# Row transfers dealt by 32 cut into four of 32 partitions, and a block's raw rows moved to another buffer, in an adaLN block with linear attention and a SiLU MLP

## The chip, the cores and the metric

The kernel runs on one core of a Trainium2 chip. Five engines work side by side, each on its own instruction stream: TensorE (PE; its weight loads are listed apart as PEld), VectorE (DVE), ScalarE (ACT), GpSimd (POOL) and SyncE (SP), which in this kernel only issues DMA transfers. Engines and transfers are tied by semaphores. The metric is the device time of one execution in microseconds (us); the median of the runs shown counts.

## The reference

All arrays are float32. With S = 2048 rows, D = 576, H = 32 heads of 18, F = 4608:

```python
mod = (_silu(c) @ w_mod).reshape(1, 6, 1, -1)
sa, ca, ga, sb, cb, gb = (mod[:, j] for j in range(6))

h = _layernorm(x) * (1 + ca) + sa
q, k, v = heads(h @ wqkv)                      # 576 -> 3 * 576
phi = lambda t: where(t > 0, t + 1, exp(t)) + 1e-6
kv  = einsum("bhsd,bhse->bhde", phi(k), v)
z   = einsum("bhsd->bhd", phi(k))
o   = einsum("bhqd,bhde->bhqe", phi(q), kv) / (einsum("bhqd,bhd->bhq", phi(q), z) + 1e-6)
x   = x + ga * (o @ wo)

h = _layernorm(x) * (1 + cb) + sb
x = x + gb * (silu(h @ w1) @ w2)               # 576 -> 4608 -> 576
```

## The kernel before, in words

**Stages.** Four stretches follow each other. From 0 to about 35 us the first 512 rows are normalised and turned, and the first modulation (sa, ca) is made. From there to about 251 us runs the *block stage*, with which most of the change has to do. To about 400 us the attention is finished and the MLP begun, and then the MLP streams its weights past two halves ("pairs") of the rows until 1125 us. The last stretch adds what is left and stores the output.

**The block stage.** The 2048 rows form four blocks of 512, and a block four tiles of 128. The rows of a block must come as columns for PE's products: element d of row s has to stand in partition d mod 128. For block 0 TensorE transposes them. For blocks 1 to 3 it goes through VectorE and DRAM (`block_steps`, from L899):

1. L902 loads four row tiles into `xt` (128 partitions x 4 x 576). They are *dealt by 32*: partition 32a + j of tile t holds row 128a + 32t + j of the block. `rows_of` (L331 to L335) gives that view of DRAM, with shape [4, 32, 576].
2. LayerNorm: statistics on DVE (L242, L243, 0.44 us each half row), small steps (L907 and L909 on DVE, a power on POOL in L908), and the normalised rows, again in `xt`: two tiles by DVE, two by ACT.
3. Four DVE transposes of 32 x 32 squares (L916), from `xt` to `sq`, which is the fourth accumulator buffer `accb[3]` ("acc" in the profile).
4. `store` (L922) writes `sq` to DRAM in four transfers; `fetch_main` (L928) and `fetch_tail` (L933) read it back, four transfers each of 32 partitions, into `xT` (in `accb[2]`) and `tail` (the profile calls it h32 or hT).
5. `turn_steps` modulates, and splits each piece into a high half (ACT, L896) and a low half (DVE, L897) in `hT`, whose products PE makes.

PE then projects k and q of the block (L846): `k_steps` gives phi(k) through an exponential on ACT (L852), L853 and L406 on DVE, and splits it into high and low parts (L861, L864). `split_rows` (L875, L877, L879) does the same with the normalised rows in `xt`, and `sum_steps` (L951) multiplies the two, summing phi(k)^T x over all rows. `xt` is therefore read until the sums' operands are split, and only then free for the next block's rows.

**The second modulation.** `mod_steps` runs beside this, once for (ga, sb) and once for the last pair: weight rows come in (L346), ACT scales them (L992, L994), POOL adds five pieces into `tmod` (L995), L996 writes the 128 partial sums to DRAM, L999 gathers them back turned (9-element runs), DVE adds them up (L1002) and L1003 writes the vector out.

**What sets the order.** The block stage is written down as a list of steps in `Schedule` (L734), each with an engine, a duration, a lag for transfers, and the names that it reads and writes. PE keeps the order of the list. On the other engines, SP among them, the planner runs the list with the given durations: the step that can begin earliest goes, and of several the one with the earliest due time. The names make the dependences: a step that writes a name comes after all that read it. `SQ` names the four parts of `sq`, `XT` those of `xT`. So the given durations change no instruction, only the order on DVE, ACT, POOL and SP. The stretch before it and the one from 251 us on have orders written out as numbers (`FIRST`, `ORDERS`): the n-th instruction of an engine within the stretch. The MLP has a planner list of its own.

**Queues.** All large transfers go out on SP's queue in order: an issue that has to wait for its data, or for a transfer issued eight earlier to land, holds up those behind it. Three other places use rows dealt by 32: q_scale (L716) and q_norm (L731), which load a tile of x into the accumulator after q has been used (12 dealt tiles of blocks 1 to 3, and 4 of block 0, which are not dealt); `store` of the MLP's first pair (L1910), half a row each; and `plain_store` (L1930) of the second pair at the end, behind `plain_add` (L1925).

Names in the profile: `big` and `small` are PSUM tiles of the first stretch, `psK` those of the projections, `psG` of the sums, `up` and `down` those of the MLP; `as_`/`a` is phi(k), `pk` its split form (shown as w in places), `xs` the split rows.

Of the kernel before, what the change touches and what calls it, by code (L numbers as in the profile page):

```python
# [18 lines left out]
P = 128  # L19
EPS_LN = 1e-5  # L20
EPS = 1e-6
# [3 lines left out]
def kernel(ctx: ExitStack, tc, A_x, A_wqkv, A_wo, B_x, B_w1, B_w2, c, w_mod, out):  # L25
# [33 lines left out]
    def behind(instructions):  # L59

        with ExitStack() as order:
# [30 lines left out]
        "SP": """  # L92
            2-4 0-1 6-7 5 8-10 13 11-12 14-16 23 20 18 17 19 25-26 22 24 21 27-30 32 31 34-35 33 38 47 37 39-40
            36 41-45 48-49 51 50 46
        """,
# [234 lines left out]

    def rows_of(y, t, c=slice(0, D)):  # L331
        b = t // 4
        if b == 0:
            return y[t * P : (t + 1) * P, c]
        return y[b * 512 : (b + 1) * 512, c].rearrange("(a t j) d -> t a j d", a=4, t=4)[t % 4]  # L335

# [374 lines left out]
    def q_scale(t, pn):  # L711
        a, r = acc[t], rs_of.pop(t)
        G.tensor_mul(pn[:, :D].rearrange("p (h d) -> p h d", d=DH), a.rearrange("p (h d) -> p h d", d=DH),
                     r.unsqueeze(2).to_broadcast([P, H, DH]))
        G.tensor_copy(pn[:, D:], pn[:, KC * P : D])
        nc.sync.dma_start(a, rows_of(x, t))  # L716

    rs_of = {}

    def q_norm(t, prod, pn):  # L720

        a = acc[t]
# [7 lines left out]
        G.tensor_copy(pn[:, D:], pn[:, KC * P : D])  # L730
        nc.sync.dma_start(a, rows_of(x, t))  # L731
        return pn
# [117 lines left out]

    def phi_steps(ps, k, out, names):
        do("ACT", 0.65, lambda: A.activation(halves(e_), ps[:, :, :HALF], AF.Exp), [k], ["e"])  # L852
        do("DVE", 0.75, lambda: V.tensor_scalar(halves(out), ps[:, :, :HALF], 0.0, EPS, op0=ALU.max, op1=ALU.add), [k], names)  # L853
        do("DVE", 0.79, lambda: phi_out(e_, out), ["e"], names)

    def k_steps(t):
        ps, k = project(t, wkp)
        i, n = t % 4, t % 2
        a, an = as_[n], f"a{n}"
        phi_steps(ps, k, a, [an])  # L860
        do("ACT", 0.68, lambda: A.copy(pk[i][:, 0], a), [an], [f"pkh{i}"])  # L861
        by_pool = i < 2 or t == 2
        eng, us = (G, 1.6) if by_pool else (V, 0.75)
        do("POOL" if by_pool else "DVE", us, lambda: eng.tensor_sub(pk[i][:, 1], a, f32(pk[i][:, 0])), [an, f"pkh{i}"], [f"pkl{i}"])  # L864
        do("POOL", 1.6, lambda: G.tensor_add(zsum, zsum, a), [an], ["zsum"])
# [5 lines left out]
    def split_rows():  # L871

        C = KC * P
        for t in range(4):
            do("ACT", 0.68, lambda t=t: A.copy(xs[t][:, :D], xt[:, t, :D]), [f"xt{t}"], [f"xhi{t}"])  # L875
            eng, us = (V, 0.7) if t < 2 else (G, 1.35)
            do("DVE" if t < 2 else "POOL", us, lambda t=t, eng=eng: eng.tensor_sub(xs[t][:, DX:], xt[:, t, :C], f32(xs[t][:, :C])),  # L877
               [f"xt{t}", f"xhi{t}"], [f"xlo{t}"])
            do("DVE", 0.17, lambda t=t: V.tensor_sub(xs[t][:, D:DX], xt[:, t, C:D], f32(xs[t][:, C:D])), [f"xt{t}", f"xhi{t}"], [f"xtl{t}"])  # L879

# [6 lines left out]
    def turn_steps(b):  # L887

        for k in START:
# [7 lines left out]
            do("DVE", 0.69, lambda src=src, lo=lo, hi=hi: V.tensor_sub(dealt(hT[b][:, lo, :]), taken(src), dealt(f32(hT[b][:, hi, :]))), [name, hs[0]], [hs[1]])  # L897

    def block_steps(b):  # L899

        for t in range(4):
            do("SP", 0.1, lambda t=t: nc.sync.dma_start(xt[:, t, :D], rows_of(x, 4 * b + t)), [], [f"xt{t}"], 6.5)  # L902
        for t in range(4):
            do("DVE", 1.1, lambda t=t: ln.stats(t, xt[:, t, :D]), [f"xt{t}"], [f"mv{t}"])
        for u in (0, 2):
            ve, rstd, nm = (t[:, u : u + 2] for t in (ln.ve, ln.rstd, ln.nm))
            do("DVE", 0.17, lambda u=u, ve=ve: V.tensor_scalar(ve, ln.mv[:, u : u + 2, 1], EPS_LN, None, op0=ALU.add), [f"mv{u}", f"mv{u + 1}"], [f"ve{u}"])  # L907
            do("POOL", 1.0, lambda u=u, ve=ve, rstd=rstd: G.tensor_tensor(rstd, ve, neghalf[:, u : u + 2], op=ALU.pow), [f"ve{u}"], [f"rstd{u}"])  # L908
            do("DVE", 0.17, lambda u=u, rstd=rstd, nm=nm: V.scalar_tensor_tensor(nm, ln.mv[:, u : u + 2, 0], -1.0, rstd, op0=ALU.mult, op1=ALU.mult), [f"rstd{u}"], [f"nm{u}"])  # L909
        for t in range(4):  # L910
            eng, us = (A, 0.86) if t % 2 else (V, 0.58)
            row = xt[:, t]
            do("ACT" if t % 2 else "DVE", us, lambda t=t, eng=eng, row=row: ln.normalise(t, row, row, eng, ((0, 0, D),)), [f"nm{t // 2 * 2}"], [f"xt{t}"])
        s3 = sq.rearrange("p (f q) -> p f q", q=P)
        for t in range(4):
            do("DVE", 0.76, lambda t=t: V.transpose(s3[:, :, 32 * t : 32 * t + 32], xt[:, t, :D].rearrange("p (f i) -> p f i", i=32)),  # L916
               [f"xt{t}"], [f"sq{t}"])
        room = turned[b - 1]
# [145 lines left out]
    def load_late():  # L1064
        for cc in range(NHC):
            n = HG if cc < NHC - 1 else TAIL
            do("SP", 0.1, lambda cc=cc, n=n: nc.sync.dma_start(wos[cc][:n], A_wo[cc * HG : cc * HG + n, :]), [], [wo_names[cc]], 6.0)
            do("DVE", 0.75, lambda cc=cc, n=n: V.tensor_mul(wos[cc][:n], wos[cc][:n], bc["ga"][:n]), ["bcga"], [wo_names[cc]])
        do("SP", 0.6, lambda: [load_rows(wvs[k], A_wqkv[:, 2 * D : 3 * D], k) for k in START], [], [*SQ, "raw1.1"], 8.0)
# [97 lines left out]
    q_steps(3)  # L1167
    turn_steps(1)
    split_rows()
    block_steps(2)  # L1170
# [4 lines left out]
    for c in START:  # L1175
        sum_steps(1, c)
    turn_steps(2)
    split_rows()
    block_steps(3)
# [583 lines left out]
    class Unit:  # L1763
# [164 lines left out]
        def plain_store(self, t, *ks):  # L1928
            a, c = 8 * self.pair + t, slice(ks[0] * HALF, (ks[-1] + 1) * HALF)
            nc.sync.dma_start(rows_of(of, a, c), acc[a][:, c])  # L1930

# [359 lines left out]
```

## Time and profile before

| what | value |
|---|---|
| runs of the kernel before | 1157.32, 1157.75, 1158.25 us (median 1157.75) |
| profiled execution, its own time | 1158.3 us |
| its span in the trace | 1156.6 us |
| mean granted TensorE clock | 0.972 |
| PE, PEld busy | 1080.4, 773.2 us |
| DVE, ACT, POOL busy | 915.8, 695.6, 722.1 us |
| moved by DMA | 193.52 MB, 167 GB/s over the span |
| block stage | 35 to 251 us |
| last stretch | 1125 to 1156.6 us |

How to read it: a group of instructions shows its line, engine, operation, tiles written and read, shape, count, then the busy time and the mean duration in ns, then the idle time of the engine just before them and what ended most of it. `SPq` is the issue of a transfer on SP's queue; its duration contains the time for which the issue stood there. A row of the chain of work gives a start, a length and what ran. A row of waits says which instruction waited on which, then the total in us, the count and the longest.

### The profile page before, as it was taken

The page shows a single profiled execution, that of the slowest core. Times are in us where ns is not written, and L with a number is a line of the kernel's source. Part 1 is how long each engine was busy: PE and PEld are TensorE (multiplying, and loading weights), DVE is VectorE, ACT ScalarE, POOL GpSimd, SP SyncE. Part 2 cuts the span into 40 slices and gives each one's busy share as a digit, 9 for nine tenths or more (in the row PEclk, how much of TensorE's full clock was granted, in tenths as well). Part 3 has the DMA queues.
Part 4 walks back from the last instruction along what each step waited for, and adds up shares of the span by engine and source line. Part 5 has one row for each costly group of instructions (what it writes and reads, how often), then busy time and mean ns, then how long its engine had stood idle before and what let it go on. Part 6 is the DMA issues. An engine that isn't in the chain of part 4 may idle for free.

```text
span 1156.6 us, 19138 instructions
## 1 busy us (share of the span) xinstructions
PE 1080.4 (93%) x7027; PEld 773.2 (67%) x7027; DVE 915.8 (79%) x1467; ACT 695.6 (60%) x1300; POOL 722.1 (62%) x789
## 2 busy tenths in 40 slices
PE   8888696999999997899999999999999999999993
PEld 7888696999888554466666666666666666666662
DVE  7768494858698889979898788887887987987672
ACT  5553334333856568767676587686676776756460
POOL 2335161435472568957979769778688777785570
PEclk9989799999999999999999999999999999999997
DMA  7353949314334575858757848747657567446312
GB/s 240 103 141 103 131 115 174 106 54 109 120 98 141 180 245 165 278 127 255 206 172 237 235 124 268 221 127 255 210 154 250 189 183 223 169 126 207 109 62 82
DMA packets 119507, 193.52 MB, mean 167 GB/s; under 512 B 42928, under 2 KB 77748, under 8 KB 119412
## 3 DMA queue, kind: packets, MB, share of 16 engines
q1 hardware_dynamic: 119240, 191.99, 56.8%
q8 instruction: 55, 0.90, 0.3%
q14 instruction: 40, 0.33, 0.1%
q10 hardware_dynamic: 172, 0.30, 0.1%
HBM read 176.77 MB, written 15.48 MB: 166 GB/s over the span
## 4 chain that ended last, share of the span: by engine, by line
PE 74%; DVE 9%; DMA 6%; ACT 4%; SPq 2%; POOL 2%; issue 1%; DVEq 0%; ACTq 0%; POOLq 0%
PE up L1803 29%; PE down L1887 28%; PE big L295 6%; PE psK L846 2%; DMA xt<-in_A_x_dram 2%; DMA acc<-turned 2%; PE psG L951 1%; PE small L1311 1%; DMA turned<-acc 1%; PE big L1322 1%; SPq L928 1%; DVE hT L167 1%; PE psK L1116 1%; DVE a L406 1%; SPq L648 1%
## 5 line engine op out<-in xcount | busy, mean ns | idle before, releaser
L1803 PE MATMUL up<-hT,w 128*128 128x512 f16 x1264 | 317.7, 381 | 8.9 <-DMA hT<-hd 4.0
L1803 PEld LDWEIGHTS <-w 128*128 128x128 f16 x1492 | 146.3, 98 | 143.5 <-issue 11.3
L1896 DVE SCALAR_TENSOR_TENSOR acc<-acc,set,down 128x576 f32<-128x576 f32 x128 | 103.5, 810 | 34.3 <-PE down L1887 33.5
L1841 POOL TENSOR_TENSOR s<-f,f 128x256 f32<-128x256 f32 x66 | 55.1, 835 | 92.8 <-ACT f L1822 90.5
L1821 ACT ACTIVATE f<-f,set 128x512 f32<-128x512 f32 x102 | 73.3, 719 | 62.2 <-DVE f L1827 51.2
L1887 PE MATMUL down<-w,hb 128*128 128x288 f16 x600 | 88.9, 286 | 2.3 <-DVE U L1898 1.7
L1887 PE MATMUL down<-w,hc 128*128 128x288 f16 x600 | 88.9, 286 | 0.2 <-DVE acc L1900 0.2
L1887 PE MATMUL down<-w,hT 128*128 128x288 f16 x480 | 82.8, 286 | 0.4 <-DVE acc L1900 0.4
L1825 DVE TENSOR_TENSOR f<-up,p 128x512 f32<-128x512 f32 x102 | 69.6, 682 | 15.0 <-PE up L1803 9.7
L1822 ACT ACTIVATE f<-f,set 128x512 f32<-128x512 f32 x102 | 73.6, 722 | 3.3
L1887 PEld LDWEIGHTS <-hb 128*128 128x128 f16 x600 | 58.7, 98 | 24.3 <-issue 2.4
L1887 PEld LDWEIGHTS <-hc 128*128 128x128 f16 x600 | 58.7, 98 | 21.9 <-issue 0.5
L846 PE MATMUL psK<-w,hT 128*128 128x288 f32 x308 | 51.9, 322 | 21.5 <-ACT hT L896 13.1
L1827 DVE TENSOR_TENSOR f<-up,f 128x512 f32<-128x512 f32 x68 | 46.8, 688 | 25.7 <-PE up L1803 25.0
L1865 POOL TENSOR_TENSOR hc<-s,hc 128x512 f16<-128x512 f32 x50 | 63.2, 1264 | 5.6 <-ACT hc L1861 5.6
L1887 PEld LDWEIGHTS <-hT 128*128 128x128 f16 x480 | 47.0, 98 | 26.6 <-issue 0.8
L1845 POOL TENSOR_TENSOR f<-f,s 128x256 f32<-128x256 f32 x66 | 53.4, 810 | 17.2 <-DVE hb L1865 10.1
L846 PEld LDWEIGHTS psK<-w,hT 128*128 128x128 f32 x308 | 48.1, 212 | 22.7 <-ACT hT L896 13.5
L1838 POOL TENSOR_TENSOR s<-f 128x256 f32<-128x256 f32 x66 | 56.6, 857 | 7.9 <-ACT f L1818 4.8
L1843 POOL TENSOR_TENSOR s<-s,f 128x256 f32<-128x256 f32 x66 | 56.2, 852 | 3.4
L951 PE MATMUL psG<-w,xs 128*128 128x288 f32 x336 | 52.3, 313 | 2.6 <-DVE sum L961 2.5
L1887 PE MATMUL down<-w,hd 128*128 128x288 f16 x396 | 54.7, 287 | 0.0
(396 smaller groups left out, 2800.5 us busy)
## 6 DMA issues: line engine op xcount, KB each, us to landing
hT<-hd SPq DMA_DIRECT2D x101, 640.0 KB
hT<-hd SPq DMA_DIRECT2D x65, 512.0 KB
hT<-in_B_w_dram SPq DMA_DIRECT2D x14, 576.0 KB
hT<-in_B_w_dram SPq DMA_DIRECT2D x28, 256.0 KB
raw<-in_B_w_dram SPq DMA_DIRECT2D x9, 576.0 KB
v<-in_B_w_dram SPq DMA_DIRECT2D x9, 576.0 KB
xt<-in_A_x_dram SPq DMA_DIRECT2D x16, 288.0 KB
raw<-in_w_mod_dram SPq DMA_DIRECT2D x8, 576.0 KB
```

The costliest lines, as they stand in the source:

```text
L295: T.matmul(ps, xpart(a), wpart(b), start=n == 0, stop=n == len(XW) - 1)
L846: T.matmul(o, part(a), w(b), start=c == 0 and m == 0, stop=c == KC and m == 1)
L951: T.matmul(ps[:, h, :HALF], l, pk[t][:, u, h * HALF : (h + 1) * HALF], start=t == 0 and m == 0, stop=t == 3 and m == len(left) - 1)
L1803: T.matmul(ps, left, right, start=first and m == 0, stop=m == len(seq) - 1, skip_group_check=True)
L1821: A.activation(f, f, AF.Silu, scale=factor(self.g, "inv"))
L1822: aside(A.activation(f, f, AF.Identity, scale=factor(self.g, "delta")))
L1825: V.tensor_add(f, self.bank[bank[1]], self.p1)
L1838: G.tensor_sub(self.s3, half(i, 0, 0), half(i, 0, 1))
L1843: G.tensor_sub(self.s[:, 1:2], self.s[:, 0:1], half(i, 0, 0))
L1865: eng.tensor_sub(t[:, :, 1, :], src, t[:, :, 0, :])
L1887: T.matmul(ps[:, p, :HALF], left[:, u, p * P : (p + 1) * P], right[:, v], start=n in (1, 5, 7, 6) and j == 0, stop=j == len(passes) - 1, s ...
L1896: V.scalar_tensor_tensor(dst, dst, factor(self.g, "ratio"), ps[:, :, :HALF], op0=ALU.mult, op1=ALU.add)
```

## The change

The kernel after differs in four ways.

- **Pieces.** `rows_of` is gone. `pieces(t, n)` gives a list of pairs: a slice of 32 partitions, and the view of 32 rows in DRAM (or n tiles' rows) that belongs there. A transfer of dealt rows becomes four transfers of 32 partitions; block 0 keeps one of 128. This holds for the loads of x in `q_scale` and `q_norm` (`load_rows_of`), and for both stores of the output. `store` of pair 0 makes one transfer (block 0) or four (block 1) for two tiles, where it made two.
- **Room.** A block's raw rows no longer go to `xt` but to `row4`, the room `accb[3]` in which the turned squares will stand, in four transfers of 32 partitions x 4 tiles. Statistics and the normalising steps read them there; the normalised rows go to `xt` as before. Each transpose now writes all four names of `SQ`, since it overwrites room of any raw tile.
- **Place in the list.** Loads and statistics form `early_steps(b)`, which stands ahead of `split_rows()` in the list, and so ahead of the last readers of the block before.
- **Durations.** The planner's figures for many steps are others. The order string of SP has new numbers for the same order, with 36 more issues.

```diff
+    def pieces(t, n=1):
+        if t < 4:
+            return [(slice(0, P), lambda y: y[t * P : (t + n) * P].rearrange("(u p) d -> p u d", u=n))]
+        r0 = [t // 4 * 512 + a * P + t % 4 * 32 for a in range(4)]
+        return [(slice(32 * a, 32 * a + 32), lambda y, r=r: y[r : r + 32 * n].rearrange("(u j) d -> j u d", u=n))
+                for a, r in enumerate(r0)]
...
-        nc.sync.dma_start(a, rows_of(x, t))
+        load_rows_of(a, t)
...
+    def load_rows_of(a, t):
+        for p, rows in pieces(t):
+            nc.sync.dma_start(a[p], rows(x)[:, 0])
...
-        do("DVE", 0.79, lambda: phi_out(e_, out), ["e"], names)
+        do("DVE", 1.05, lambda: phi_out(e_, out), ["e"], names)
...
-        eng, us = (G, 1.6) if by_pool else (V, 0.75)
+        eng, us = (G, 1.52) if by_pool else (V, 1.1)
...
-            eng, us = (V, 0.7) if t < 2 else (G, 1.35)
+            eng, us = (V, 0.74) if t < 2 else (G, 1.55)
...
-    def block_steps(b):
+    def early_steps(b):
+        row4 = accb[NB - 1]
+        def load():
+            for p, rows in pieces(4 * b, 4):
+                nc.sync.dma_start(row4[p], rows(x))
+        do("SP", 0.3, load, [], SQ, 7.0)
         for t in range(4):
-            do("SP", 0.1, lambda t=t: nc.sync.dma_start(xt[:, t, :D], rows_of(x, 4 * b + t)), [], [f"xt{t}"], 6.5)
-        for t in range(4):
-            do("DVE", 1.1, lambda t=t: ln.stats(t, xt[:, t, :D]), [f"xt{t}"], [f"mv{t}"])
+            do("DVE", 1.1, lambda t=t: ln.stats(t, row4[:, t]), [f"sq{t}"], [f"mv{t}"])
...
+    def block_steps(b):
+        row4 = accb[NB - 1]
         for t in range(4):
-            eng, us = (A, 0.86) if t % 2 else (V, 0.58)
-            row = xt[:, t]
-            do("ACT" if t % 2 else "DVE", us, lambda t=t, eng=eng, row=row: ln.normalise(t, row, row, eng, ((0, 0, D),)), [f"nm{t // 2 * 2}"], [f"xt{t}"])
+            eng, us = (A, 0.87) if t % 2 else (V, 0.7)
+            do("ACT" if t % 2 else "DVE", us, lambda t=t, eng=eng: ln.normalise(t, xt[:, t], row4[:, t], eng, ((0, 0, D),)),
+               [f"nm{t // 2 * 2}", f"sq{t}"], [f"xt{t}"])
...
-               [f"xt{t}"], [f"sq{t}"])
+               [f"xt{t}"], SQ)
...
-        do("SP", 0.4, store, SQ, [f"turned{b}"], 4.7)
-        do("SP", 0.4, fetch_main, [f"turned{b}"], XT, 4.5)
-        do("SP", 0.4, fetch_tail, [f"turned{b}"], [XTAIL], 5.5)
+        do("SP", 0.4, store, SQ, [f"turned{b}"], 5.2)
+        do("SP", 0.4, fetch_main, [f"turned{b}"], XT, 5.0)
+        do("SP", 0.4, fetch_tail, [f"turned{b}"], [XTAIL], 6.0)
...
+    early_steps(1)
     split_rows()
     block_steps(1)
...
+    early_steps(2)
     split_rows()
     block_steps(2)
...
+    early_steps(3)
     split_rows()
     block_steps(3)
...
-            for u in range(2):
-                nc.sync.dma_start(rows_of(of, 4 * b + 2 * i + u, slice(k * HALF, (k + 1) * HALF)), self.c(b, i, k)[:, u])
+            for p, rows in pieces(4 * b + 2 * i, 2):
+                nc.sync.dma_start(rows(of[:, k * HALF : (k + 1) * HALF]), self.c(b, i, k)[p])
...
-            nc.sync.dma_start(rows_of(of, a, c), acc[a][:, c])
+            for p, rows in pieces(a):
+                nc.sync.dma_start(rows(of[:, c])[:, 0], acc[a][p, c])
```

In the order that the planner then writes, PE's instructions stand as before. Rows of block 1 are issued right behind the startup's last weight load (L302) and ahead of the weight rows of L648; those of blocks 2 and 3 right behind the fetch of the block before. The gather L999 (L1019 in the kernel after) of the first `mod_steps` is issued ahead of the second block's store instead of behind it, and on DVE the first statistics of blocks 2 and 3 stand ahead of some low halves of `hT`.

More of the change, by code (lines that the diff above doesn't have):

```diff
@@ L92 @@
         "SP": """
-            2-4 0-1 6-7 5 8-10 13 11-12 14-16 23 20 18 17 19 25-26 22 24 21 27-30 32 31 34-35 33 38 47 37 39-40
-            36 41-45 48-49 51 50 46
+            2-4 0-1 6-13 5 14-25 28-31 26-27 32-43 50-53 47 45 44 46 55-62 49 54 48 63-66 68 67 70-71 69 74 83
+            73 75-76 72 77-81 84-85 87 86 82
         """,
@@ L730, in q_norm @@
         G.tensor_copy(pn[:, D:], pn[:, KC * P : D])
-        nc.sync.dma_start(a, rows_of(x, t))
+        load_rows_of(a, t)
         return pn
@@ L849, in project, with phi_steps @@
         return ps, k
-    def phi_steps(ps, k, out, names):
+    def phi_steps(ps, k, out, names, by_act=False):
         do("ACT", 0.65, lambda: A.activation(halves(e_), ps[:, :, :HALF], AF.Exp), [k], ["e"])
-        do("DVE", 0.75, lambda: V.tensor_scalar(halves(out), ps[:, :, :HALF], 0.0, EPS, op0=ALU.max, op1=ALU.add), [k], names)
-        do("DVE", 0.79, lambda: phi_out(e_, out), ["e"], names)
+        if by_act:
+            do("ACT", 0.65, lambda: A.activation(halves(out), ps[:, :, :HALF], AF.Relu), [k], names)
+            do("ACT", 0.68, lambda: A.activation(out, out, AF.Identity, bias=eps), [], names)
+        else:
+            do("DVE", 0.75, lambda: V.tensor_scalar(halves(out), ps[:, :, :HALF], 0.0, EPS, op0=ALU.max, op1=ALU.add), [k], names)
+        do("DVE", 1.05, lambda: phi_out(e_, out), ["e"], names)
+    BY_ACT = ()
     def k_steps(t):
@@ L875, in split_rows @@
             do("ACT", 0.68, lambda t=t: A.copy(xs[t][:, :D], xt[:, t, :D]), [f"xt{t}"], [f"xhi{t}"])
-            eng, us = (V, 0.7) if t < 2 else (G, 1.35)
+            eng, us = (V, 0.74) if t < 2 else (G, 1.55)
             do("DVE" if t < 2 else "POOL", us, lambda t=t, eng=eng: eng.tensor_sub(xs[t][:, DX:], xt[:, t, :C], f32(xs[t][:, :C])),
                [f"xt{t}", f"xhi{t}"], [f"xlo{t}"])
-            do("DVE", 0.17, lambda t=t: V.tensor_sub(xs[t][:, D:DX], xt[:, t, C:D], f32(xs[t][:, C:D])), [f"xt{t}", f"xhi{t}"], [f"xtl{t}"])
+            do("DVE", 0.3, lambda t=t: V.tensor_sub(xs[t][:, D:DX], xt[:, t, C:D], f32(xs[t][:, C:D])), [f"xt{t}", f"xhi{t}"], [f"xtl{t}"])
     def dealt(y):
@@ L1067, in load_late @@
             do("SP", 0.1, lambda cc=cc, n=n: nc.sync.dma_start(wos[cc][:n], A_wo[cc * HG : cc * HG + n, :]), [], [wo_names[cc]], 6.0)
-            do("DVE", 0.75, lambda cc=cc, n=n: V.tensor_mul(wos[cc][:n], wos[cc][:n], bc["ga"][:n]), ["bcga"], [wo_names[cc]])
+            do("DVE", 1.1, lambda cc=cc, n=n: V.tensor_mul(wos[cc][:n], wos[cc][:n], bc["ga"][:n]), ["bcga"], [wo_names[cc]])
         do("SP", 0.6, lambda: [load_rows(wvs[k], A_wqkv[:, 2 * D : 3 * D], k) for k in START], [], [*SQ, "raw1.1"], 8.0)
```

11 lines of the change are left out of this document (3 added, 8 removed).

## The prediction

> **What bounds the kernel now.** I read the page first, then the busy time by stage, PE's own waits, the chain of work in order of time, and the queue of SP. The page:
>
> ```profile
> span 1156.6 us, 19138 instructions
> PE 1080.4 (93%) x7027; PEld 773.2 (67%) x7027; DVE 915.8 (79%) x1467; ACT 695.6 (60%) x1300; POOL 722.1 (62%) x789
> PE up L1803 29%; PE down L1887 28%; PE big L295 6%; PE psK L846 2%; DMA xt<-in_A_x_dram 2%; DMA acc<-turned 2%; PE psG L951 1%; PE small L1311 1%; DMA turned<-acc 1%; PE big L1322 1%; SPq L928 1%; DVE hT L167 1%; PE psK L1116 1%; DVE a L406 1%; SPq L648 1%
> ```
>
> PE is the bound, but the chain also holds transfers: rows of x, the turned squares. By stage (length; busy us and instructions of PE, PEld, DVE, ACT, POOL; granted clock; DMA share; GB/s):
>
> ```profile
> 35.00:81.00 46.00, 38.36 (x252) 37.54 (x252) 28.77 (x53) 19.13 (x31) 16.05 (x10) 0.89 0.52 142
> 81.00:135.00 54.00, 38.42 (x256) 37.30 (x256) 33.40 (x49) 18.86 (x28) 16.12 (x10) 0.85 0.66 110
> 135.00:180.60 45.60, 41.60 (x288) 40.43 (x289) 36.45 (x58) 19.96 (x29) 25.42 (x14) 0.95 0.54 140
> 180.60:216.40 35.80, 27.63 (x176) 26.93 (x176) 22.86 (x33) 18.12 (x34) 14.43 (x11) 0.86 1.01 175
> 1125.00:1156.60 31.60, 11.92 (x96) 9.29 (x95) 9.49 (x19) 3.81 (x6) 4.61 (x3) 0.73 0.21 75
> ...
> PE psK L846 <- ACT hT L896: 13.1, 2, 10.0
> PE psK L846 <- ACT e L852: 7.5, 1, 7.5
> PE psG L951 <- DVE w L864: 5.8, 3, 4.2
> PE psG L951 <- ACT w L861: 2.9, 2, 2.4
> ```
>
> PE idles in the block stage (35 to 216) and at the end. The second group is PE's waits from 30 to 251: for a block's turned rows (3.1, then 10.0 us), once for an exponential, and for the parts of k.
>
> The chain tells why (start, length):
>
> ```profile
> 42.02 11.63 DMA xt<-in_A_x_dram
> 67.41 5.08 DMA turned<-acc
> 73.83 5.55 DMA acc<-turned
> 81.01 5.55 PE psK L846 x28
> 105.48 2.67 DVE acc L916 x4
> 115.81 8.31 SPq L928
> 125.11 6.13 DMA acc<-turned
> 145.87 11.30 DMA xt<-in_A_x_dram
> 162.33 2.02 DVE acc L916 x3
> ```
>
> A dealt row transfer takes 11 us; turning (L916) follows, then a round trip through DRAM, then PE.
>
> **The change, part by part.** PE's order stays as it was; DVE, ACT and POOL have the same instructions in another order; SP issues 67 transfers more (53 become 120). Times below are those of the profiled execution.
>
> *Rate.* Two stretches, one with the 32-partition fetches of L928 in flight, one with only the dealt stores of L1930:
>
> ```profile
> 73.00:79.00 6.00, 4.91 (x37) 4.68 (x36) 1.43 (x3) 2.03 (x4) 2.63 (x2) 1.00 0.95 209
> 1141.50:1155.00 13.50, 0.00 (x0) 0.00 (x0) 0.00 (x0) 0.00 (x0) 0.00 (x0) 0.50 0.25 96
> ```
>
> The dealt form keeps a quarter of the 16 DMA engines busy and moves 96 GB/s; 32-partition transfers keep 0.95 busy at 209. So I price the pieces at 209: a block's four transfers, 1.18 MB, take 5.6 us instead of 12.3 (their bounds). The Trainium skill ("DMA: Bandwidth & Descriptors", on why a DMA increments its semaphore by 16) says that a transfer runs on the largest number of engines up to 16 that divides its slowest dimension, four here; the share of 0.25 agrees. Against the change, "SBUF — State Buffer" (the DMA port swizzle) says that 32 partitions reach 8 of the 16 ports and gives 189 GB/s; by it a block would take 6.2 us, and the sum be 0.6 us smaller.
>
> *Step 1, block 1.* Its rows went to xt and waited for xt's readers; now they go to acc3, unused so far, behind the last weight load, in the place of L648:
>
> ```profile
> 20.86 0.75 SPq L648 DMA_DIRECT2D acc<-in_B_w_dram  x1
> 74.31 1.82 SPq L933 DMA_DIRECT2D h<-turned x4
> ...
> 53.67 0.82 DVE L242 BATCH_NORM_STATS2 st<-xt 128x6 f32<-128x288 f32 x2 [4.33 <-DMA xt<-in_A_x_dram]
> ...
> L406 DVE SCALAR_TENSOR_TENSOR a<-e,a 128x576 f32<-128x576 f32 x15 | 16.2, 1080 | 1.1 <-ACT e L852 0.7
> L853 DVE TENSOR_SCALAR a<-psK 128x576 f32<-128x576 f32 x14 | 10.4, 744 | 5.6 <-ACT e L852 3.3 <-POOL v L877 1.2 <-PE psK L846 1.1
> L242 DVE BATCH_NORM_STATS2 st<-xt 128x6 f32<-128x288 f32 x24 | 9.7, 444 | 6.3 <-DMA xt<-in_A_x_dram 6.3
> L916 DVE STREAM_TRANSPOSE acc<-xt 128x576 f32<-128x576 f32 x12 | 8.4, 743 | 0.0
> ```
>
> They land near 32, before DVE wants them (41.2), so its wait of 4.33 goes, and with it what it delayed in DVE's order (k of tile 3, for which PE waited: L861, L864). From 41.2 DVE does four statistics (2 x 0.44 and some 0.2 for the aggregate), three each of L853 (0.74) and L406 (0.7 without the waits in its mean), some 3.5 us of small ones: 12.2 us, to 53.4; with about 2.9 us of waits for the third k tile and for POOL the turning starts at 56.3 and, 4 x 0.74 later, ends at 59.3. Before, it ended 2.3 ahead of the last store's issue at 67.41, at 65.1. From there to PE at 81.01 lie 15.9 us, unchanged. PE itself would be free earlier (two waits of 3 us go). Gain 5.8; ends 4.3 (the one wait) and 9 (all of PE's waits here, and its slow start after them).
>
> *Step 2, block 2* (times without step 1). Now the rows leave right behind L933 (76.1) and need acc3, free once stored. They queue behind the fetches (landing 79.4) and land near 86. Their first statistic stands in DVE's order ahead of two of the five low halves of hT, so DVE stands from 83.5 to 86 and PE loses some 2 us: a new wait, but PE waits for the next block anyway. The turning ends at 105 instead of 108.15. The other half is the gather of the summed modulation (L999), which SP issued between store and fetch:
>
> ```profile
> 101.35 0.60 SPq L996 DMA_DIRECT2D parts<-tmod  x1
> 111.87 1.30 SPq L999 DMA_DIRECT2D raw<-parts  x1
> 185.89 0.39 SPq L999 DMA_DIRECT2D raw<-parts  x1
> 186.37 10.98 SPq L648 DMA_DIRECT2D acc<-in_B_w_dram  x2
> ```
>
> Whatever SP issues behind it is stuck for 11 to 12 us (to 124.12, to 197.35). It now stands ahead of the store: POOL's last add of tmod precedes two sums of z, which lets L996 go at about 92, the gather at 95, and frees the queue at 106.5 to 107. The store goes then, not at 105; 7.4 us to landing and 6.9 for the fetch make 121.3, against 131.24. Gain 9.9; ends 4.9 (the gather 5 us later, all of it before the store) and 12 (it is out of the way; PE's sums then end last, near 119.6).
>
> *Step 3, block 3* (from the fetch's landing H). Before, the turning ended at H+33.1 (164.35). Now the rows land at H+6.5, DVE stands 4 us with four low halves behind it, PE loses 2.7; but the 11 us wait at the row transfer goes, and the turning, held by k tiles 8 to 11 and q tile 5, ends at H+31.5. PE's sums end at H+49, after the turned rows (H+47.3): no wait, 4 us better than before. Then PE waits again, for the second gather: tile 13's L853 stands behind its reduction on DVE, and the 7.5 us above is that. The gather hangs on block 3's store by SP's order: 1.6 earlier, and an L406 that stood before the reduction no longer does, 0.7. So only 2.3 of the 4 stays. Ends: -3 (the statistics' stand grows) and 7.5 (the whole wait).
>
> *Step 4, the stores at the end.*
>
> ```profile
> 1128.01 17.99 SPq L1930 DMA_DIRECT2D out_dram<-acc  x9
> L1930 SPq DMA_DIRECT2D out_dram<-acc x9: 537/598/5286, 1128.0 to 1140.7; - x9
> 1136.49 1.13 DVE L1925 SCALAR_TENSOR_TENSOR acc<-up,set,acc 128x288 f32<-128x288 f32 x2
> SPq L2286 <- DMA out_dram<-acc: 9.1, 1, 9.1
> ...
> SPq L663 <- DMA limits<-hT: 3.4, 1, 3.4
> ...
> SPq L731 <- POOL pn L730: 58.4, 10, 16.0
> ```
>
> DVE ends at 1137.62, SP at 1146.0, the last store lands at 1155.1: 2.4 MB at 96 GB/s. Now 36 pieces leave; L933's four took 0.46 each. Data at 209 GB/s (0.35 a piece) is faster than that, so SP's issue is late next: 1128.0 + 36 x 0.47 = 1144.9. A small store lands at most 3.4 after its issue; I take 1.7, halfway, and the last 1.5 us of the span stay: 1148.1. Gain 8.5; ends 3.8 (0.6 an issue, the median of L1930) and 10.5 (issue hidden, 0.41).
>
> *At no cost.* Behind 251 rows of x go as 48 pieces instead of 12: 48 x 0.47 less 12 x 0.56 is 16 us more on SP, under 58.4 us in which it waits for POOL there. If that cover goes, the weight loads behind it are late. New planner durations cost nothing but order. Fewer, larger stores of blocks 0 and 1 take as many issues.
>
> *Sum.* 5.8 + 9.9 + 2.3 + 8.5 = 26.5. The profiled execution took 1158.3 (span and 1.7 around it), 0.55 over the median 1157.75: 1131.8, or 1131 as a median.
>
> **The rivals.** (a) *The gather eats block 2.* If L996 goes later than 92, the store waits behind the whole gather, and only 3 of 9.9 and nothing of step 3 stays: 5.8 + 3 + 8.5 = 17.3, 1140.5. For it: POOL waits for ACT's scaling before each such add. Against: POOL is busy 16 of 54 us there. (b) *The change doesn't do what it says*: pieces move at 96 GB/s. Then rows land 6.7 later, step 2 falls to 3.5, step 3 to -4.4, the tail to 0, step 1 holds by its slack: 5 gained, 1153. The share of 0.95 speaks against it. (c) *Slower*: at the end SP's queue gets stuck on 36 pieces as it did on L1930 (the longest 5.29). With 18 us from steps 1 to 3 it decides from 1128 + 36p + 3.2 = 1174.6, p = 1.21 us; at 1.5 the time is 1168. Against: 0.46 with eight in a row of L928 and L933.
>
> **How the numbers follow.** Forecast 0.60, (a) 0.22, (b) 0.11, (c) 0.05, no change 0.02. The forecast's own range is 1123 to 1140. For 8 in 10 I take 1119 (upper ends of steps 1 to 4: 39) to 1146, which takes in (a) and leaves out (b) and (c). About 0.2% is what a measurement can tell here; faster 0.92, same 0.03, slower 0.05.
>
> **What would show it.** Right: no wait of DVE for rows before 60; the gather issued before the second store; PE's wait for the third block's hT (10.0) at half or less, none for the fourth; a wait for the second gather still there; the last store landing within 4 us of its issue. Wrong: DVE standing over 5 us at a statistic, L942 stuck for 10 us, or pieces over 0.6 us of issue each.

## The result, and the profile after

The kernel after runs in 1147.2 us (median, 1145.7 to 1151.6), the kernel before beside it in 1157.5. The ratio is 0.9916, with an interval of 0.9888 to 0.9943: about 10 us faster, not 26.5. The profiled execution took 1145.7 us, 12.6 less than that of before. Its page:

```profile
span 1144.0 us, 19228 instructions
PE 1081.1 (95%) x7027; PEld 773.8 (68%) x7027; DVE 927.1 (81%) x1467; ACT 695.5 (61%) x1300; POOL 722.1 (63%) x789
```

DVE has the same 1467 instructions as before, and is busy 11.3 us longer. Most of that lies in the block stage: from 36 to 216 us it is 129.9 us in 189 instructions, where it was 120.1 us in 187. That is the first sign of what went wrong. PE's own waits from 30 to 256 us:

```profile
PE psK L851 <- DVE hT L908: 10.9, 5, 4.6
PE psK L851 <- DVE a L862: 7.9, 2, 6.0
PE psK L851 <- ACT hT L907: 5.1, 2, 3.0
PE psG L971 <- DVE w L875: 4.3, 3, 3.1
```

The wait of 10.0 us for the third block's turned rows has become 2.1 (two waits for L907, 5.1 in all, the longer one of 3.0 at the fourth block, where the forecast had none). In its place PE waits 10.9 us for L908, the low halves of `hT`, which it hardly did before.

Where the 12.6 us come from is read off two groups of products that have the same place in PE's order in both kernels, one at the start of the block stage and one near its end, and off SP's queue at the end. The two rows of before, from the timeline of PE:

```profile
36.37 4.99 PE L846 MATMUL psK<-wq,hT 128*128 128x288 f32 x24 [2.02 <-DVE a L402]
...
229.72 3.36 PE L846 MATMUL psK<-wq,hT 128*128 128x288 f32 x24
```

The same of the kernel after, then rows of its SP queue:

```profile
37.66 4.99 PE L851 MATMUL psK<-wq,hT 128*128 128x288 f32 x24 [2.02 <-DVE a L403]
...
227.87 3.36 PE L851 MATMUL psK<-wq,hT 128*128 128x288 f32 x24
...
19.22 3.43 SPq L916 DMA_DIRECT2D acc<-in_A_x_dram  x4
93.07 0.39 SPq L1019 DMA_DIRECT2D raw<-parts  x1
107.21 0.34 SPq L347 DMA_DIRECT2D raw<-in_w_mod_dram  x1
110.73 3.56 SPq L942 DMA_DIRECT2D turned<-acc  x4
187.42 0.39 SPq L1019 DMA_DIRECT2D raw<-parts  x1
1124.34 17.59 SPq L1954 DMA_DIRECT2D out_dram<-acc  x36
```

The block stage gives 1.85 us (3.1 if the later start at 37.66 is taken off), where steps 1 to 3 promised 18. From there to the first store at the end (1128.01 before, 1124.34 after) another 1.8 us came, in the streaming part. The end itself went from 28.6 us (1128.01 to 1156.6) to 19.7 (1124.34 to 1144.0): 8.9, where step 4 said 8.5.

Inside the block stage DVE and POOL show what happened. From the timelines of the two engines, after:

```profile
54.88 4.57 DVE L259 TENSOR_SCALAR xt<-acc,mv 128x576 f32<-128x576 f32 x2
54.90 1.43 POOL L876 TENSOR_TENSOR zsum<-zsum,a 128x576 f32<-128x576 f32 x1
56.29 2.83 POOL L1015 TENSOR_TENSOR tmod<-tmod,raw 128x1152 f32<-128x1152 f32 x1
...
83.39 0.82 DVE L242 BATCH_NORM_STATS2 st<-acc 128x6 f32<-128x288 f32 x2 [1.49 <-DMA acc<-in_A_x_dram]
84.37 2.65 DVE L908 TENSOR_TENSOR hT<-acc,hT 128x512 fp32r<-128x512 f32 x1
86.95 3.10 DVE L908 TENSOR_TENSOR hT<-h,hT 128x512 fp32r<-128x512 f32 x1
83.86 5.63 POOL L1015 TENSOR_TENSOR tmod<-tmod,raw 128x1152 f32<-128x1152 f32 x2 [5.57 <-ACT raw L1014]
```

Two normalising steps, which take 0.57 us each where nothing disturbs them (e3 below), took 4.57, until POOL's two additions had ended. Two low halves behind the statistic of the next block took 2.65 and 3.10 instead of 0.69, each until one of POOL's two additions ended. The same stretch once more in front of the third turning:

```profile
124.75 1.00 DVE L267 TENSOR_SCALAR acc<-acc,col_a 128x512 f32<-128x512 f32 x2 [5.20 <-DMA acc<-turned]
131.08 0.82 DVE L242 BATCH_NORM_STATS2 st<-acc 128x6 f32<-128x288 f32 x2 [4.06 <-DMA acc<-in_A_x_dram]
151.10 2.95 DVE L407 SCALAR_TENSOR_TENSOR a<-e,a 128x576 f32<-128x576 f32 x1
156.89 2.70 DVE L925 SCALAR_TENSOR_TENSOR mv<-mv 128x2 f32<-128x2 f32 x2
162.92 2.76 DVE L936 STREAM_TRANSPOSE acc<-xt 128x576 f32<-128x576 f32 x4
...
150.79 2.64 POOL L1015 TENSOR_TENSOR tmod<-tmod,raw 128x1152 f32<-128x1152 f32 x1
156.60 2.90 POOL L1015 TENSOR_TENSOR tmod<-tmod,raw 128x1152 f32<-128x1152 f32 x1 [3.16 <-ACT raw L1014]
```

L925 works on 128x2 elements and took 2.70 us for two. The third turning ended at 165.7, that is 40.9 us behind the landing of the turned rows of block 2 (L267 at 124.75). The forecast had 31.5; before it was 33.1.

### The profile page after: what moved, and what is told of

Same layout as the page of the kernel before. It is cut to its first block, busy times and chain, and to the rows that moved or that the text cites. A ratio compares the mean times of both kernels' runs of the same rounds, so it can differ in the third digit from the quotient of the medians.

```text
span 1144.0 us, 19228 instructions
## 1 busy us (share of the span) xinstructions
PE 1081.1 (95%) x7027; PEld 773.8 (68%) x7027; DVE 927.1 (81%) x1467; ACT 695.5 (61%) x1300; POOL 722.1 (63%) x789
## 4 chain that ended last, share of the span: by engine, by line
PE 73%; DVE 9%; DMA 7%; POOL 4%; ACT 3%; issue 2%; SPq 1%; DVEq 0%; POOLq 0%; ACTq 0%
PE up L1826 28%; PE down L1910 28%; PE big L295 7%; PE psK L851 3%; DMA acc<-turned 2%; PE small L1334 1%; PE psG L971 1%; DMA turned<-acc 1%; PE big L1345 1%; DMA raw<-parts 1%; DVE xt L259 1%; PE psK L1136 1%; DVE acc L936 1%; DVE a L407 1%; PE big L1259 1%
## 5 line engine op out<-in xcount | busy, mean ns | idle before, releaser
L851 PE MATMUL psK<-w,hT 128*128 128x288 f32 x308 | 54.5, 330 | 20.4 <-DVE hT L908 9.2
L1910 PE MATMUL down<-w,ha 128*128 128x288 f16 x396 | 54.4, 286 | 0.1
```

Source lines behind the costliest of these rows:

```text
L851: T.matmul(o, part(a), w(b), start=c == 0 and m == 0, stop=c == KC and m == 1)
L1910: T.matmul(ps[:, p, :HALF], left[:, u, p * P : (p + 1) * P], right[:, v], start=n in (1, 5, 7, 6) and j == 0, stop=j == len(passes) - 1, s ...
```

## The experiments

Three theories stood against each other. LOCK: DVE stands while POOL reads SBUF. ORDER: the next block's statistics stand ahead of low halves. GATHER: the second gather sets the time at k tile 14, which PE starts at 203 us in both kernels after a wait (7.5 us before, 6.0 after), whatever came before. The kernel before ran beside each group again, with medians of 1157.5 to 1159.8, so gains are taken against the one beside.

| kernel | us | ratio to before (interval) | gain, us |
|---|---|---|---|
| after | 1147.2 | 0.9916 (0.9888 to 0.9943) | 10.3 |
| e1 tails alone | 1150.4 | 0.9938 (0.9922 to 0.9955) | 8.0 |
| e2 before, POOL sums thinned | 1148.7 | 0.9925 (0.9901 to 0.9949) | 9.7 |
| e3 after, POOL sums thinned | 1128.9 | 0.9745 (0.9731 to 0.9760) | 29.5 |
| e4 statistics behind | 1137.7 | 0.9826 (0.9808 to 0.9843) | 20.7 |
| e5 memsets in POOL | 1130.6 | 0.9756 (0.9720 to 0.9791) | 27.7 |
| e6 old durations | 1147.9 | 0.9914 (0.9889 to 0.9940) | 10.4 |
| e7 gather first | 1148.1 | 0.9912 (0.9887 to 0.9937) | 10.2 |
| e8 two queues | 1139.5 | 0.9837 (0.9812 to 0.9862) | 18.8 |
| e9 no tails | 1154.3 | 0.9976 (0.9958 to 0.9993) | 3.5 |
| e10 loads dealt | 1146.9 | 0.9901 (0.9882 to 0.9920) | 10.8 |
| e11 behind and queues | 1131.2 | 0.9767 (0.9749 to 0.9785) | 26.5 |
| e12 sums on DVE | 1136.0 | 0.9813 (0.9792 to 0.9834) | 21.8 |
| e13 tmod sum thinned | 1134.2 | 0.9780 (0.9760 to 0.9800) | 25.6 |
| e14 thinned and behind | 1122.9 | 0.9683 (0.9662 to 0.9703) | 36.9 |
| e15 POOL in parts | 1128.8 | 0.9733 (0.9689 to 0.9776) | 31.0 |

### e1 and e9: the end alone, and all but the end

e1 is the kernel before with `store` and `plain_store` of the kernel after; e9 is the reverse (its `plain_store` is shown; `store` goes back in the same way):

```diff
-            for p, rows in pieces(a):
-                nc.sync.dma_start(rows(of[:, c])[:, 0], acc[a][p, c])
+            nc.sync.dma_start(rows_of(of, a, c), acc[a][:, c])
```

> The kernel before with the two output stores alone made in pieces (store and plain_store); loads, rooms, list and durations stay as they were. Three theories are tested in this study. LOCK: what steps 1 to 3 promised was lost because DVE instructions that take both inputs from SBUF stood until a POOL addition that was running had ended (L908 took 2.65 and 3.10 us in the changed kernel, 0.69 without POOL). ORDER: it was lost because the statistics of the next block stand ahead of low halves of hT on DVE, and wait for rows. GATHER: PE starts k tile 14 at 203 us in both kernels because the second gather, issued behind the third block's store, sets that time whatever came before. For this run all three say the same: step 4 is worth 8.9 us (28.59 us from the first L1930 to the end of the span before, 19.66 after), so 1148.6, between 1147.5 and 1150. If it gives under 6 us, the end of the changed kernel is worth more than its own edit and step 4 was only right by chance.

> The changed kernel with the two output stores dealt as before: steps 1 to 3 alone. The stores alone gave 8.0 us (1150.4 against 1158.4); if the parts add up, this kernel stands where the changed one stands less that: 1155, between 1153.5 and 1157, and steps 1 to 3 are worth 2 to 3 us of the 18 that were forecast. Under 1152 would say that the parts do not add.

They gave 8.0 and 3.5 us, together 11.5, against 10.3 for both. The parts add within their intervals: step 4 is right, and steps 1 to 3 are worth 3.5 of 18.

### e2, e3 and e13: POOL's additions made short

```diff
-G.tensor_add(dst, dst, raw[:kp])
+G.tensor_add(dst[:, :, 0:8], dst[:, :, 0:8], raw[:kp, :, 0:8])
...
-G.tensor_add(zsum, zsum, a)
+G.tensor_add(zsum[:, 0:8], zsum[:, 0:8], a[:, 0:8])
```

> The kernel before, with POOL's additions of tmod and of the sum of phi(k) made on 8 columns only (the rest of these two sums is left out); list, durations and order are unchanged. POOL's 2.7 and 1.4 us instructions become short ones. LOCK: DVE stands less, above all L406 (3.24 at its longest), L864 and L909; the first parts store goes some 2.7 us earlier and with it the fetch of block 2 behind the gather: 1149 to 1155. ORDER and GATHER: little beyond the 2.7 us of the earlier gather: 1153 to 1158.

> The changed kernel with the same two sums thinned in the same way. LOCK: block 1's normalising on DVE takes 1.2 instead of 4.57 us, the low halves of block 1 some 1.4 instead of 5.65, and the turning of block 3 ends some 7 us sooner; 1131 to 1138, that is 15 to 24 us under the thinned kernel before. ORDER: the low halves wait for rows as before; at most 4 us gained, 1143 to 1147, the gap to the thinned kernel before stays at 10 to 13. GATHER: the turning of block 3 moves, and the second gather with it; without LOCK it does not move.

The thinned kernel after is 19.8 us under the thinned kernel before, twice the gap of the whole ones (10.3). It gained 19.2 us by thinning, the kernel before 9.7. Both times lie a little beyond LOCK's ranges (1149 to 1155, 1131 to 1138) and clear of ORDER's (1153 to 1158, 1143 to 1147). In e3 (a row of all normalising steps on DVE with their shortest, median and longest ns; then two of DVE's timeline; below, the same row of the kernel after):

```profile
L259 DVE TENSOR_SCALAR xt<-acc,mv x6: 566/568/575, 55.3 to 145.5; 128x576 f32<-128x576 f32 x6
115.35 1.00 DVE L267 TENSOR_SCALAR acc<-acc,col_a 128x512 f32<-128x512 f32 x2 [5.47 <-DMA acc<-turned]
146.15 2.76 DVE L936 STREAM_TRANSPOSE acc<-xt 128x576 f32<-128x576 f32 x4
```

```profile
L259 DVE TENSOR_SCALAR xt<-acc,mv x6: 569/1698/2871, 54.9 to 161.1; 128x576 f32<-128x576 f32 x6
```

The rows of block 2 land at 115.35 here, where the forecast's steps 1 and 2 put them (121.3 less 5.8 is 115.5), and the third turning ends 33.6 us behind instead of 40.9. The forecast's arithmetic was that of a kernel in which POOL doesn't hold DVE. Thinning also lets the first parts store go earlier (at 83.51 instead of 89.53). That is not what brought the second block's store forward: in both kernels it left with DVE's last transpose (110.73 behind 110.70, in e3 101.25 behind 101.22).

> The changed kernel with the sum of tmod alone thinned to 8 columns (the rest of that sum is left out); the sum of phi(k) is whole. LOCK by length: the long additions (2.7 us) hold most, 1.4 us ones little: 12 to 15 of the 18.3 us that both gave, 1132 to 1135. LOCK by count: there are 9 additions of tmod and 15 of the other sum in the block stage; if what counts is how often a DVE instruction meets one, half: 1137 to 1140. Over 1143 would say that the sum of phi(k) is what holds.

With only the 2.7 us additions thinned 15.3 us of the 19.2 are there. The long instructions hold most.

### e5: POOL kept busy without reading

```diff
-G.tensor_add(dst, dst, raw[:kp])
+(G.memset(dst, 0.01), G.memset(dst, 0.01), G.tensor_add(dst[:, :, 0:8], dst[:, :, 0:8], raw[:kp, :, 0:8]))
...
-G.tensor_add(zsum, zsum, a)
+(G.memset(zsum, 1.0), G.memset(zsum, 1.0), G.tensor_add(zsum[:, 0:8], zsum[:, 0:8], a[:, 0:8]))
```

> The changed kernel with the same two sums left out as in the thinned kernel (additions on 8 columns), but POOL stays busy in their place: two memsets of the same tile stand ahead of each, which write SBUF and read nothing. LOCK says that it is POOL's reading of SBUF that makes DVE stand: the time is that of the thinned kernel (1128.9) plus at most 3, 1128 to 1132, and normalising on DVE takes 0.57 us each again. The rival QUEUE says that DVE does not stand for POOL's reads; POOL's own short steps (the powers of L924) and its low halves were late behind the long additions, and thinning freed them: with memsets of about 1 us each in their place 1138 to 1146.

1130.6: as in the thinned kernel, though POOL spends 2.4 us on memsets in place of each addition of `tmod`; from 36 to 216 us it is busy 69.2 us, against 71.7 in the kernel after and 37.8 in e3. QUEUE falls. The memsets need not wait for ACT's scaled rows, so POOL is done sooner after these rows come, and that alone could have helped QUEUE's short steps; but in the kernel after all of DVE's waits for POOL in this stretch come to 0.4 us (`DVE mv L925 <- POOL mv L924: 0.4, 1, 0.4`). One part of the expectation was wrong, though:

```profile
54.19 2.37 POOL L1015 MEMSET tmod<- 128x1152 f32 x2
...
53.53 2.03 DVE L259 TENSOR_SCALAR xt<-acc,mv 128x576 f32<-128x576 f32 x2
55.48 0.74 DVE L875 TENSOR_TENSOR w<-a,w 128x576 fp32r<-128x576 f32 x1
```

L875, with two inputs in SBUF, ran through in the middle of the memsets at its undisturbed 0.74. The normalising L259, with one, took 2.03 for two instead of 1.14: the memsets still held it.

### e4: the statistics behind the low halves

```diff
-lambda t=t: ln.stats(t, row4[:, t]), [f"sq{t}"], [f"mv{t}"])
+lambda t=t: ln.stats(t, row4[:, t]), [f"sq{t}", *(f"h{(b - 1) % 2}.{k}b" for k in START if b > 1)], [f"mv{t}"])
```

> The changed kernel, with the statistics of blocks 2 and 3 made to wait in the planner's list for the low halves of hT of the block before (a name more in what they read; no semaphore more, both are on DVE). ORDER: PE's waits for L908 (10.9 us in all, 8.5 of it for low halves that stood behind a statistic) go, and 5 to 8 us are gained: 1139 to 1142. LOCK: the halves that POOL held are still partly under its additions, and the DVE chain to the turning of block 3 is still held for some 8 us: 0 to 3 us gained, 1144 to 1147. GATHER: PE still waits at tile 14 for the reduction of the second gather; unless the third block's store goes earlier nothing is gained.

It gained 10.4 us over the kernel after, above ORDER's 5 to 8. PE's waits for L908 are out of its list, and the third store leaves at 154.85 instead of 165.70, which moves the second gather with it, as GATHER asked. PE still waits for it at tile 14, 8.6 us, but starts that tile at 192.20 instead of 203.05:

```profile
PE psK L851 <- DVE a L862: 15.2, 4, 8.6
...
154.85 3.56 SPq L942 DMA_DIRECT2D turned<-acc  x4
171.61 0.58 SPq L1016 DMA_DIRECT2D parts<-tmod  x1
```

### e14: both causes away

> The changed kernel with both causes taken away: both sums thinned (rest left out) and the statistics behind the low halves. If LOCK and ORDER are separate costs they add: 18.3 and 9.5 us, 1119 to 1121. If ORDER cost what it did only because the low halves slid under POOL's additions, it is worth 2 to 4 us without them: 1124 to 1128.

1122.9. The statistics are worth 7.4 us without the holds (36.9 less 29.5) and 10.4 with them, so the two causes are separate but for some 3 us: neither branch of the expectation was met. Set against e2, the kernel before with the same sums thinned, the change now gives 27.2 us (36.9 less 9.7), close to the 26.5 forecast. Less the 8.0 of the stores (e1) that leaves 19.2 for steps 1 to 3, where 18 was forecast and e9 got 3.5.

### e6 and e10: the planner's figures, the loads behind 251 us

e6 puts all durations back; e10 loads the rows of x dealt again, `nc.sync.dma_start(a, rows_of(x, t))`, in `q_scale` and `q_norm`.

> The changed kernel with the planner's durations and lags of the kernel before put back (the room, the pieces, the place in the list stay). If the new figures only moved orders by little, 1144 to 1150 as the changed kernel has. LOCK and ORDER both say that what DVE meets is set by small shifts: the statistics of blocks 2 and 3 stand between low halves here too (behind one and three of them), so ORDER says the same 1145 to 1150; LOCK gives no number better than within 6 us of 1147. Under 1140 would say that the durations are what cost the change its gain.

> The changed kernel with the 12 dealt loads of x behind 251 us (q_norm, q_scale) made in one transfer each again, so that SP has 36 issues fewer there. The prediction put the pieces at no cost and no gain there, under SP's waits for POOL: 1145.5 to 1149, as the changed kernel (1147.2). Lower than 1144 would say that the 36 issues cost something; over 1150 that the faster loads are worth something.

1147.9 and 1146.9. Neither the new figures nor the 36 issues did anything that can be measured.

### e7: the second gather first

```diff
-do("SP", 0.1, load, [], room, 8.0)
+do("SP", 0.1, load, ["raw0.0", "raw1.0"], room, 8.0)
```

> The changed kernel with the second parts store and gather issued directly behind the third block's fetch, ahead of the six loads of L649 that now stand before it (a name more in what these loads read in the list). In the trace the parts store would leave at 176.6 instead of 183.17, and the reduction end at 195.8 instead of 202.3. GATHER: the 6 us for which PE waits at tile 14 go: 1141 to 1142.5. If loads of the scan, now behind the gather, are what PE meets next, 1143 to 1146. If PE's wait hangs on DVE and not on the gather, 1146 to 1148.

1148.1, no gain, at the edge of the last branch. Two waits of PE behind tile 14 that the kernel after does not have, and a row of DVE:

```profile
211.22 0.85 PE L971 MATMUL psG<-w,v 128*128 128x288 f32 x2 [2.02 <-ACT w L872]
214.21 1.33 PE L971 MATMUL psG<-w,v 128*128 128x288 f32 x4 [2.14 <-DVE w L875]
...
209.03 0.76 DVE L1088 TENSOR_TENSOR xt<-xt,bc_ga 126x576 f32<-126x576 f32 x1 [1.87 <-DMA xt<-in_A_wo_dram]
```

The wait at tile 14 fell from 6.0 to 3.0. But loads of `wo` came late, their scaling L1088 stood on DVE ahead of phi(k) and its low parts, and PE waited 2.0 us for the high parts of k and 2.1 for the low ones. Other waits took the place of the first.

### e8 and e11: the last stores on two queues

```diff
-            for p, rows in pieces(a):
-                nc.sync.dma_start(rows(of[:, c])[:, 0], acc[a][p, c])
+            for u, (p, rows) in enumerate(pieces(a)):
+                (nc.scalar if u % 2 else nc.sync).dma_start(rows(of[:, c])[:, 0], acc[a][p, c])
```

> The changed kernel with every second piece of the last stores issued by ACT instead of SP. Step 4 said that SP's issues, not the data, end the span (36 at 0.47 us, the last landing 1.6 after its issue). If so 18 on each queue keep up with DVE, whose last addition ends at 1133.9, and the last piece lands near 1137 instead of 1143: 6 to 7 us less, 1140 to 1141.5. If the data at 158 GB/s were the bound, nothing much changes: 1145 to 1147. If two issuing engines slow each other down, in between.

> The changed kernel with the two edits that gained most together: statistics of blocks 2 and 3 behind the low halves, and every second piece of the last stores on ACT. They act 900 us apart, so they should add: 1147.2 less 9.5 less 7.7, that is 1130, between 1128 and 1132.5.

```profile
1122.91 11.26 SPq L1954 DMA_DIRECT2D out_dram<-acc  x18
```

In e8 the span ends at 1136.5, 13.6 us behind the first of these stores instead of 19.7: 6.1 us, so SP's issues were what ended the span, as step 4 said. The median gained 8.5 us, with intervals of some 3 us on both sides; in the trace the block stage, which the edit doesn't touch, was 3.3 us shorter as well (186.9 us between the two groups of products, 190.2 in the kernel after). e11, with the edit of e4, gave 1131.2, within its range; its gain is 26.5, where 10.3, 10.4 and 8.5 add to 29.2.

### e12 and e15: versions with shorter holds

e12 makes the sum of `tmod` on DVE; e15 leaves it on POOL in instructions of 288 columns, and the sum of phi(k) too. Both stand on e11.

```diff
-do("ACT", 1.25, lambda raw=raw, kp=kp, scale=scale: A.activation(raw[:kp], raw[:kp], AF.Identity, scale=scale), [], raws2[i])
-do("POOL", 2.7, lambda raw=raw, dst=dst, kp=kp: G.tensor_add(dst, dst, raw[:kp]), raws2[i], ["tmod"])
+do("DVE", 1.4, lambda raw=raw, dst=dst, kp=kp, scale=scale: V.scalar_tensor_tensor(
+    dst, raw[:kp], scale, dst, op0=ALU.mult, op1=ALU.add), raws2[i], ["tmod"])
```

> The kernel of the run before this one, and the sums of tmod made by DVE (one multiply-add of 128x1152 each, some 1.4 us, in place of ACT's scaling and POOL's addition of 2.7 us), so that the longest POOL reads are gone and the result stays complete. LOCK: DVE gets 8 x 1.4 = 11 us more to do, half of it in its idle stretches, and loses the holds by these additions (normalising 4.6 to 1.2, several of 2 us each on the way to the third turning): 4 to 9 us less, 1121 to 1126. If the additions on DVE cost what the holds cost, 1129 to 1132.

1136.0, 5 us slower than e11 and outside both branches. The holds did get shorter (the mean of L407 is 759 ns, 1179 in e11), but the planner, with other work on DVE, issued the first gather behind the second block's fetch, and DVE stood at its reduction, ahead of phi(k):

```profile
119.79 0.43 SPq L1019 DMA_DIRECT2D raw<-parts  x1
...
136.45 2.19 DVE L1022 TENSOR_REDUCE crow<-raw 128x9 f32<-128x1152 f32 x1 [8.10 <-DMA raw<-parts]
```

> The kernel with the statistics behind and the last stores on two queues (1131.2), with POOL's two sums made in instructions of 288 columns (four for tmod, two for the sum of phi(k)) instead of 1152 and 576; the result is complete. By the POOL rows one of 288 takes some 0.9 us, so an addition of tmod takes 3.6 instead of 2.7 us in all. LOCK: DVE stands until the running instruction ends, now at most 0.9 us instead of 2.7: 3 to 8 us less, 1123 to 1128. If DVE cannot get in between two POOL instructions, or if POOL's longer sums are what counts, 1131 to 1135.

1128.8 (1124.0 to 1133.5), against 1131.2. The groups of POOL from 36 to 215 us, first of e15, then of the kernel after:

```profile
L1015 POOL TENSOR_TENSOR tmod<-tmod,raw 128x288 f32<-128x288 f32 (+1 forms) x32 | 29.1, 942 | 13.2 <-ACT raw L1014 13.2
```

```profile
L1015 POOL TENSOR_TENSOR tmod<-tmod,raw 128x1152 f32<-128x1152 f32 (+1 forms) x8 | 22.8, 2850 | 28.0 <-ACT raw L1014 28.0
```

Taken against the kernels before beside them that is 4.5 us more than e11, in the lower half of LOCK's 3 to 8; by the times themselves it is 2.4, between the two branches, and a spread of 9.5 us leaves open how much of it is sure. The shorter instructions did not always let DVE in. The mean of the normalising steps L259 fell from 1438 ns in e11 to 1016, but that of L407 stayed (1179, 1172), and once it stood while three instructions of POOL followed each other:

```profile
95.50 3.12 DVE L407 SCALAR_TENSOR_TENSOR a<-e,a 128x576 f32<-128x576 f32 x1
...
95.07 1.55 POOL L876 TENSOR_TENSOR zsum<-zsum,a 128x288 f32<-128x288 f32 x2
96.58 1.42 POOL L875 TENSOR_TENSOR w<-a,w 128x576 fp32r<-128x576 f32 x1
```

e15 is the fastest version here whose result is complete, at 0.9733 of the kernel before; e11 at 0.9767 is not told apart from it.

## Why the prediction was wrong

The range ended at 1146 and the time was 1147.2; the gain was 10, not 26.5. Against the forecast's own steps:

- **Rate: right as a time.** Block 1's rows, issued from 19.22, were there before DVE wanted them; DVE has no wait for rows before 60 us. A block's rows followed the fetch by some 6.3 us (fetch at 124.75, first statistic at 131.08), where 6.5 was said. The 209 GB/s behind it was not that of 32-partition transfers alone: from 76.23 dealt rows of L902 were under way in the same stretch.
- **Step 1, 5.8 forecast: 2.4 in place.** The last store of block 1 left at 65.03 instead of 67.41, or 3.7 earlier against the stage's start, which was 1.3 later. What failed is the walk along DVE's instructions at their short durations: L406 was priced "0.7 without the waits in its mean", and the normalising steps stood among "some 3.5 us of small ones"; only 2.9 us were allowed for waits, POOL among them. The surplus in such a mean (1.08 against some 0.75) was POOL holding the instruction, and it didn't vanish; it passed to what came next in the order, two normalising steps at 4.57 us.
- **Step 2, 9.9 forecast, 15.7 with step 1: 6.5 in all.** The turned rows of block 2 landed at 124.75 instead of 131.24. The gather left at 93.07 (95 forecast), and the store at 110.73, behind DVE's last transpose and not behind the gather. So rival (a) did not happen, although its time, 1140.5, was nearer. That the queue was free at 107.2, as forecast (106.5 to 107), was luck: the issue behind the gather, L347, stood for ACT, which was still reading its room (`SPq L347 <- ACT tmod L1012: 11.9, 1, 11.9`). DVE's stand at the first statistic was foreseen with a loss of 2 us for PE; the low halves behind it then slid under POOL's additions, for which PE waited 3.9 and 1.7 us. With the 4.6 behind the third block's statistic, where step 3 had 2.7, L908 cost PE 10.9 us in all.
- **Step 3, 2.3 forecast: this is where the gains of steps 1 and 2 were lost.** The turning came at 40.9 instead of 31.5 us from the landing, 7.8 later than before, so that tile 14 waited for a second gather issued at 187.42 instead of 185.89. The wait was foreseen; that the gather would be no earlier was not. What failed is again the price of DVE's chain, with POOL's holds put at nothing, and the price of the statistics' place: the 40.9 become 33.6 with POOL's sums thinned (e3), 35.7 with the statistics behind (e4, 119.1 to 154.8) and 28.2 with both (e14, 114.1 to 142.3).
- **Step 4, 8.5 forecast: 8.9 in the trace, 8.0 in the medians of e1.** 36 issues at 0.49 us, and the last store landed 1.6 behind its issue.
- **At no cost: right** (e10, e6), though the stores of blocks 0 and 1 take 20 issues, not the 16 of before.

The forecast said that DVE "standing over 5 us at a statistic" or pieces over 0.6 us would make it wrong. Neither came. The cause had no rival of its own: an engine holding another. It was in the rows that were read. The means of L406 (1080), quoted in the prediction, and of L853 (744), an instruction of the same shape with its input in PSUM, differ by 0.34 us, and POOL was busy 14 to 25 us of each stretch of the block stage.

Shown: thinning POOL's sums doubles what the change is worth (e2, e3), and it is POOL's reading that does most of it (e5). Shown too: the statistics' place cost 7 to 10 us (e4, e14), where PE's loss had been put at 2 and 2.7. The 1.8 us of the streaming part and the later start of the block stage say nothing about the change: from the second group of products to the first store at the end it is 898.3 us before, 896.5 after, and 896.2 to 899.7 in the traces of e1 to e15; and the first group starts at 36.4 before, 37.7 after, and between 35.8 and 40.6 in the others. The kernel after also varies by 6 us between executions. That fits a race between DVE and POOL instructions that start close together, but it was not tested.

## What to carry to other kernels

Compare the mean of a DVE group with that of the same shape reading PSUM, or with its shortest: what is over is likely time under a POOL instruction, it counts as busy and not as idle, and a reordering hands it to whatever DVE does next. So price a moved chain with the holds that wait at its new place, and look there for long POOL instructions. Where an engine stands in order behind a transfer, put first what others wait for.

## What the runs showed of the hardware

In the block stage of the kernel after, DVE instructions with two inputs in SBUF (L407, L908, and L925 even at 128x2) stood up to 2.5 us until a running POOL addition ended (the longest L925 took 2.63, the shortest 0.15). Those with an input from PSUM (L862, none over 0.76) and the transposes (none over 0.78) were never held. The Trainium skill ("SBUF — State Buffer", on who interferes with whom) says that DVE and GpSimd share a second pair of ports as an exclusive lock for the whole instruction, that two SBUF inputs collide only with GpSimd instructions that read SBUF, and a fast-mode `tensor_scalar` with any. e5 agrees on both: beside memsets L875 kept its 0.74 us, and L259 took 2.03 for two. That L259 runs in such a mode is inferred: undisturbed it takes 0.57 us, where L862, of the same shape out of PSUM, takes 0.75. The prediction had used that page for the DMA ports alone.

Issuing is a limit of its own: 36 pieces of 32 partitions took 17.59 us on one queue, 0.49 each, and the whole end 6.1 us less when a second engine issued half of them.
